# A mixture-of-experts kernel: three copies of each branch instead of five, and five branches an expert instead of eight

## The chip, the cores and the metric

The kernel runs on one core of a Trainium2 chip. TensorE (PE) multiplies matrices, VectorE (DVE), ScalarE (ACT) and GpSimd (POOL) work element by element, SyncE (SP) issues most transfers. The metric is the time of one execution on the device in microseconds, the median of several runs.

## The reference, cut to what matters

Attention with a decay writes one row of 512 values for each of 4608 tokens; each token then goes to one of eight experts, and the expert's two matrix products are done for its tokens alone:

```python
logits = x @ w_gate
expert_idx = np.argmax(logits, axis=1)
...
for e in range(E):
    mask = expert_idx == e
    xe = x[mask]
    h = np.maximum(xe @ w1[e], 0.0)      # 512 -> 1024
    ye = h @ w2[e]                       # 1024 -> 512
    out[mask] = gate_w[mask, None] * ye
```

How many tokens an expert gets is known only on the chip, since the routing depends on the data.

## The kernel before, in words

The first part of the program is the attention; the rest is the experts, one after the other. Each expert has room for CAP = 640 tokens. Expert 0 is done in a simpler way, partly beside the attention's end; experts 1 to 7 all run the same code, and the change touches these seven.

An expert from 1 to 7 has two stages. In the **up stage** (line 1421) the first product, xe @ w1, is done by a seven-product scheme for 2 x 2 blocks (Strassen's): the tokens are split in even and odd ones, 320 columns each, and the sums of blocks that the scheme needs are made beforehand (names T1 to T4, B11, B21, B22). The hidden width of 1024 is cut into four **groups** i = 0..3, and each group needs seven products s = 0..6, so an expert has 28 products, numbered 0 to 27 here (product 7i+s). A product is six matmuls of 128 x 128 weights against n columns (the values are held as a high and a low part, hence three matmuls for each of two halves of the inner dimension), so the up stage has 168 matmuls. In the **down stage** (line 1229) the second product follows in five tiles of 128 tokens with 24 matmuls of 512 columns each; the tiles of the next expert's tokens are turned between them (line 1390).

The number of columns n depends on the expert's token count. `arms` turns the count into a number from 0 to ARMS-1, TensorE loads it into a register at the start of the expert (`begin_up`), and `by_count` writes a tree of branches whose ends hold one whole copy of the same matmuls for each n:

```python
def pick(lo, hi):
    if lo == hi:
        f(HN - ARM * lo)          # one copy, with HN - ARM * lo columns
        return
    mid = (lo + hi + 1) // 2
    with self.tc.If(self.arm < mid) as branch:
        pick(lo, mid - 1)
    with branch.Else():
        pick(mid, hi)
```

Only the copy that is taken runs; the code of the others is jumped over. The first matmul that opens a bank has 320 columns in every copy (16 of the 168). With this data the experts 1 to 7 run with 320, 320, 288, 304, 256, 304 and 288 columns.

A branch comes with the products 0 to 3 of each group, and another with the products 4 to 6, so TensorE goes through eight trees an expert, with borders at the products 0, 4, 7, 11, 14, 18, 21 and 25.

The other engines turn a group's banks into the hidden layer (`after`, `end`, `last`): ACT copies bank a to p1 (line 1475) and bank g to p5 (line 1481); DVE adds u2 = b + p1 (line 1478), then u3 (1486), d (1487), g (1494); POOL adds p5 (1488); ACT takes relu of each (`relu`, line 1466, into hhw) and DVE the low part (`rest`, line 1469, into hl). They work at the full 320 columns whatever n is. Between these stand the tasks for the same engines: rounding and splitting the weights of this expert and the next (lines 1333, 1339, 1348, 1349), sums of weight blocks on POOL (1318 to 1321), loads and gathers. Every engine has its own queue, and the instructions keep the order in which the program lists them; semaphores tie the engines together. A group's last sums and relus (`ends`) are listed after the next group's first products, those of the last group at the start of the down stage.

Of the kernel before, what the change touches and what calls it, by code (L numbers as in the profile page):

```python
# [9 lines left out]
F32 = mybir.dt.float32  # L10
# [5 lines left out]
ALU = mybir.AluOpType  # L16
# [4 lines left out]
P = 128  # L21
# [3 lines left out]
D = H * HD  # L25
# [12 lines left out]
FT = FF // P  # L38
# [2 lines left out]
CA, CB = NA * P, NB * P  # L41

HN = CAP // 2
ARM, ARMS = 16, 5
XM = 2 * (KT // 2) * HN
XN = ("T2", "T1", "T4", "T3", "B22")

# [126 lines left out]
def psum(pool):  # L174
    return pool.tile([P, 512], F32, name="ps", tag="ps")
# [13 lines left out]
def attention_all(c, tc, qkT, va, vb, f, wgd, x_dram, batch_done, more_consts, extra):  # L189
# [659 lines left out]
    def run(f):  # L849
        step(f)  # L850
        order.pin()

    return run, todo


# [213 lines left out]
class Moe:  # L1069
# [69 lines left out]
    def fetch(self, e, m):  # L1139

        c, nc = self.c, self.nc
        early = e == 0 and m < NA
        gi, s = (self.idx["early"], m) if early else self.index(e, m)[::3]
        rows = self.x_dram
        if early:
            rows = rows[0 : rows.shape[0] - LATE * S]

        xg = c.rows.tile([P, D], F32R, name="xg", tag="row")
        nc.gpsimd.indirect_dma_start(
            out=xg.bitcast(F32), out_offset=None, in_=rows,  # L1150
            in_offset=bass.IndirectOffsetOnAxis(ap=gi[:, s : s + 1], axis=0),
        )
        self.xg[e, m] = xg
# [289 lines left out]
            max_val=ARMS - 1,  # L1443
        )

    def seven(self, e, i, run, tasks):

        c, nc = self.c, self.nc
        V, A, G = nc.vector, nc.scalar, nc.gpsimd
        pools = (c.ps_t, c.ps_t, c.ps_m, c.ps_v) if i % 2 == 0 else (c.ps_s,) * 3  # L1450
        a, b, g, d = [psum(p) for p in pools] + [c.ps_r] * (i % 2)
        a, b, g, d = (t[:, 0:HN] for t in (a, b, g, d))

        late = (e, i) == (1, 0)
        p1, p5, u2, u3 = (
            c.yp.tile([P, D], F32, name="y")[:, 0:HN] if late and k == 1
            else c.values["u", k] if k < 2 else self.up_.tile([P, HN], F32, name=f"u{k}")
            for k in range(4)
        )
        hh, hl = self.h[e]  # L1460

        def place(h, f, n):
            return h[:, f * (FT // 2) + i].rearrange("p (s j) -> p j s", j=2)[:, n]

        def relu(src, *at):
            A.activation(place(hh, *at), src, AF.Relu)  # L1466

        def rest(src, *at):
            V.scalar_tensor_tensor(place(hl, *at), src, 0.0, place(hh, *at).bitcast(F32),  # L1469
                                   ALU.max, ALU.subtract)  # L1470

        def after(s):
            if s == 0:
                self.ends.pop(0)()
                A.copy(p1, a)
                self.ends.pop(0)()
            elif s == 1:
                V.tensor_tensor(u2, b, p1, ALU.add)
                self.ends.pop(0)()
            elif s == 2:  # L1480
                A.copy(p5, g)  # L1481
            elif s == 4:
                relu(a, 0, 0)
                rest(a, 0, 0)
            elif s == 5:
                V.tensor_tensor(u3, b, p1, ALU.add)  # L1486
                V.tensor_tensor(d, u3, d, ALU.subtract)
                G.tensor_tensor(p5, u3, p5, ALU.add)  # L1488

        def end():  # L1490
            relu(d, 1, 0)
            if not late:
                relu(p5, 1, 1)
            V.tensor_tensor(g, g, u2, ALU.add)
            rest(d, 1, 0)

        steps = ((a, 0, 0, "B11", True), (b, 0, 1, "T2", True), (g, 0, 2, "T1", True),
                 (d, 0, 3, "T4", True), (a, 1, 0, "B21", False), (b, 1, 1, "T3", False),
                 (g, 1, 2, "B22", False))
        for some in ((0, 1, 2, 3), (4, 5, 6)):  # L1500
            run(lambda: self.by_count(
                e, lambda n: [self.product(e, i, n, *steps[s]) for s in some]))
            for s in some:
                run(lambda: after(s))
                for f in tasks.get(7 * i + s, []):
                    run(f)
        def last():
            if late:
                relu(p5, 1, 1)
            rest(p5, 1, 1)  # L1510
            rest(g, 0, 1)

        self.ends = [end, lambda: relu(g, 0, 1), last]

    def run(self, run, tasks):
        c, tc = self.c, self.tc
# [4 lines left out]
        def downs(e, ms, tasks):  # L1521
            k = 0
            for m in ms:
                for q in range(4):
                    run(lambda: self.down(e, m, (2 * q, 2 * q + 2)))
                    for f in tasks.get(k, []):
                        run(f)
                    k += 1
# [27 lines left out]
        with tc.tile_pool(name="moe_h", bufs=1) as hp, tc.tile_pool(name="moe_u", bufs=1) as up_, \  # L1556
                tc.tile_pool(name="moe_r", bufs=2) as self.wr:
            self.up_ = up_
            hl = hp.tile([P, FT * CAP], F32R, name="hl")
            h = [t.rearrange("p (f s) -> p f s", s=CAP) for t in (c.words["hh"], hl)]  # L1560
            G = self.nc.gpsimd
            for e in range(1, E):
                self.h[e] = h
                run(lambda: self.begin_up(e))
                S = lambda f, *args: T(f, e, *args)
                N = lambda f, *args: T(f, e + 1, *args)
                ups, dns = {}, {}

                def at(d, *items):
                    for k, f in items:  # L1570
                        d.setdefault(k, []).append(f)

                late = 9 if e == 1 else 1
                at(ups, (0, S(self.load_v, 0)), (0, S(self.load_v, 1)),
                   (4, S(self.round_s, 2, 1)), (6, S(self.rest_s, 2, 1, G)),
                   (late, S(self.load_v, 2)), (late, S(self.load_v, 3)),
                   (8, S(self.split_s, 3, 0)), (11, S(self.round_s, 3, 1)),
                   (13, S(self.rest_s, 3, 1, G)))
                for i, k in enumerate((15, 22, 16, 23) if e == 1 else (9, 15, 16, 22)):
                    at(ups, (k, S(self.split_v, i)))  # L1580
                if e == 1:
                    at(ups, (0, S(self.sums_s, 3)), (2, S(self.split_s, 2, 0)))
                if e + 1 < E:
                    at(ups, (9, N(self.load_s, 0)), (16, N(self.load_s, 1)),
                       (6, fetch(e + 1, 3)), (6, fetch(e + 1, 4)), (13, fetch(e + 1, 2)),
                       (20, N(self.sums_s, 0)), (20, fetch(e + 1, 0)),
                       (27, N(self.sums_s, 1)))
                    at(dns, (0, N(self.begin_t)), (0, N(self.turn_t, 3)), (0, fetch(e + 1, 1)),
                       (0, N(self.split_s, 0, 0)), (1, N(self.split_s, 0, 1)),
                       (2, N(self.load_s, 2)), (2, N(self.turn_t, 4)),  # L1590
                       (3, N(self.split_s, 1, 0)), (4, N(self.turn_t, 2)),
                       (5, N(self.split_s, 1, 1)), (6, N(self.load_s, 3)),
                       (6, N(self.turn_t, 0)), (7, N(self.sums_s, 2)),
                       (8, N(self.turn_t, 1)), (9, N(self.split_s, 2, 0)),
                       (10, N(self.split_t, "T2")), (11, N(self.split_t, "T1")),
                       (12, N(self.split_t, "T4")), (13, N(self.split_t, "T3")),
                       (14, N(self.sums_s, 3)))
                else:
                    at(ups, (27, lambda: tc.keep_in_program_order(G.drain())))
                self.ends = [lambda: None] * 3  # L1600
                for i in range(FT // 2):
                    self.seven(e, i, run, ups)
                dns.setdefault(0, [])[:0] = self.ends
                downs(e, range(NST), dns)

# [222 lines left out]
```

## Time and profile before

| | |
|---|---|
| time, median of 3 runs | 767.41 us (767.35 to 769.39) |
| the profiled execution | 766.13 us, of it a span of 764.4 us |
| PE busy | 741.7 us, 97% of the span |
| DVE, POOL, ACT busy | 541.7, 513.3 and 499.3 us |
| up stages of experts 1 to 7, together | 181.49 us |
| down stages of the same | 217.10 us |

The span is the time from the first to the last instruction that the profiler recorded; 1.7 us of the time lie outside it. "Busy" adds up the time in which an engine has an instruction in work; matmuls overlap each other in the records, so two that follow without a pause start closer together than one of them lasts.

### The profile page before, as it was taken

The page shows a single profiled execution, that of the slowest core. Times are in us where ns is not written, and L with a number is a line of the kernel's source. Part 1 is how long each engine was busy: PE and PEld are TensorE (multiplying, and loading weights), DVE is VectorE, ACT ScalarE, POOL GpSimd, SP SyncE. Part 2 cuts the span into 40 slices and gives each one's busy share as a digit, 9 for nine tenths or more (in the row PEclk, how much of TensorE's full clock was granted, in tenths as well). Part 3 has the DMA queues.
Part 4 walks back from the last instruction along what each step waited for, and adds up shares of the span by engine and source line. Part 5 has one row for each costly group of instructions (what it writes and reads, how often), then busy time and mean ns, then how long its engine had stood idle before and what let it go on. Part 6 is the DMA issues. An engine that isn't in the chain of part 4 may idle for free.

```text
span 764.4 us, 18736 instructions
## 1 busy us (share of the span) xinstructions
PE 741.7 (97%) x6464; PEld 633.3 (83%) x6464; DVE 541.7 (71%) x1596; ACT 499.3 (65%) x1319; POOL 513.3 (67%) x681
## 2 busy tenths in 40 slices
PE   9999999999999999999989999999999889999996
PEld 5888888888888887989978888988988878978985
DVE  6668898988888887627777387486585585685720
ACT  6999998999899996525555465464554554653621
POOL 6999998989898989544864475465565465565311
PEclk8999999999999999999999999999999999999998
DMA  6957787777766674333533613622632532623200
GB/s 187 222 151 211 197 215 189 204 198 212 202 197 213 200 217 139 111 117 110 182 95 111 199 53 111 206 67 90 204 96 93 170 93 83 193 83 108 77 29 34
DMA packets 78583, 112.17 MB, mean 147 GB/s; under 512 B 9327, under 2 KB 40047, under 8 KB 78448
## 3 DMA queue, kind: packets, MB, share of 16 engines
q1 hardware_dynamic: 71408, 90.38, 41.6%
q0 software_dynamic: 6400, 19.93, 8.0%
q8 instruction: 91, 1.49, 0.8%
q14 instruction: 44, 0.36, 0.2%
q10 hardware_dynamic: 640, 0.01, 0.0%
HBM read 91.26 MB, written 20.07 MB: 146 GB/s over the span
## 4 chain that ended last, share of the span: by engine, by line
PE 85%; DVE 6%; POOL 4%; issue 2%; ACT 1%; DMA 1%; SPq 0%; POOLq 0%; DVEq 0%; ACTq 0%
PE ps L1229 29%; PE ps L1421 13%; PE ps L525 11%; PE ps L402 9%; PE ps L454 8%; PE ps L436 4%; PE ps L1195 3%; PE ps L449 3%; DVE w_1w L1349 2%; DVE hl L1469 2%; PE ps L1390 1%; PE ps L616 1%; POOL u L1488 1%; POOL w L1086 1%; ACT hhw L1466 1%
## 5 line engine op out<-in xcount | busy, mean ns | idle before, releaser
L421 ACT ACTIVATE sc<-sc,nmx 128x512 f32<-128x512 f32 (+3 forms) x256 | 142.4, 559 | 5.6 <-DVE nmx L378 4.6
L1238 POOL DMA_INDIRECT out<-y,si_fast x40 | 42.9, 1072 | 118.0 <-ACT y L1237 75.0
L1229 PE MATMUL ps<-w_0w,hhw 128*128 128x512 f32 x280 | 113.4, 405 | 2.6 <-ACT hhw L1466 2.6
L1229 PE MATMUL ps<-w_0w,hl 128*128 128x512 f32 x280 | 110.7, 395 | 0.0
L1229 PE MATMUL ps<-w_1w,hhw 128*128 128x512 f32 x280 | 110.3, 394 | 0.0
L1421 PE MATMUL ps<-X_0w,w1s 128*128 128x320 f32 (+3 forms) x504 | 107.3, 304 | 0.2 <-ACT u L1481 0.2
L466 ACT COPY aT<-ps 128x512 f32<-128x512 f32 (+1 forms) x224 | 93.3, 506 | 1.9 <-PE ps L454 1.1
L329 POOL TENSOR_TENSOR hl<-raw,hl 128x640 fp32r<-128x640 f32 (+1 forms) x60 | 89.7, 1494 | 5.0
L525 PE MATMUL ps<-aT,va_t 128*64 128x256 f32 (+3 forms) x896 | 90.3, 353 | 0.0
L1421 PEld LDWEIGHTS ps<-X_0w,w1s 128*128 128x128 f32 x504 | 83.2, 191 | 0.5 <-ACT u L1481 0.4
L1237 ACT ACTIVATE y<-ps,g_fast 128x512 f32<-128x512 f32 x40 | 27.6, 689 | 81.2 <-PE ps L1229 81.2
L402 PE MATMUL ps<-hl 64*128 64x512 f32 (+1 forms) x720 | 79.8, 339 | 0.0
L525 PEld LDWEIGHTS ps<-aT,va_t 128*64 128x64 f32 x896 | 56.1, 137 | 28.5 <-issue 5.0
L1421 PE MATMUL ps<-X_1w,w1s 128*128 128x320 f32 (+3 forms) x252 | 76.0, 301 | 0.3 <-issue 0.3
L1488 POOL TENSOR_TENSOR u<-u,u 128x320 f32<-128x320 f32 x27 | 23.8, 881 | 68.3 <-DVE u L1486 60.3
L1421 PE MATMUL ps<-xa,w1s 128*128 128x320 f32 (+3 forms) x336 | 58.4, 310 | 11.0 <-issue 3.5
L378 DVE CUSTOM_DVE_ANT_0 sc<-ps,bias 128x128 f32<-128x128 f32 (+1 forms) x128 | 59.8, 486 | 10.3 <-PE ps L402 3.7
L1229 PEld LDWEIGHTS ps<-w_0w,hhw 128*128 128x128 f32 x280 | 52.5, 187 | 14.8 <-ACT hhw L1466 4.5
L1229 PEld LDWEIGHTS ps<-w_0w,hl 128*128 128x128 f32 x280 | 52.6, 188 | 14.1 <-DVE hl L1469 1.7
L1421 PEld LDWEIGHTS ps<-xa,w1s 128*128 128x128 f32 x336 | 50.2, 193 | 15.6 <-issue 4.8
L1229 PEld LDWEIGHTS ps<-w_1w,hhw 128*128 128x128 f32 x280 | 52.7, 188 | 10.1
L378 DVE CUSTOM_DVE_ANT_1 sc<-ps,bias 128x256 f32<-128x256 f32 (+1 forms) x128 | 57.7, 487 | 3.4 <-PE ps L402 3.3
(247 smaller groups left out, 1886.7 us busy)
## 6 DMA issues: line engine op xcount, KB each, us to landing
bias<-ud SPq DMA_DIRECT2D x30, 576.0 KB, 5.9
w1r<-in_w SPq DMA_DIRECT2D x112, 128.0 KB, 2.6
w<-in_w SPq DMA_DIRECT2D x28, 512.0 KB, 5.1
raw<-in_qkT SPq DMA_DIRECT2D x64, 160.0 KB, 3.6
raw<-in_qkT SPq DMA_DIRECT2D x64, 144.0 KB, 3.6
va_t<-in_va SPq DMA_DIRECT2D x32, 256.0 KB, 5.7
x_dram<-row SPq DMA_DIRECT2D x32, 256.0 KB, 2.7
wraw<-in_w SPq DMA_DIRECT2D x7, 512.0 KB, 3.9
```

The lines of the kernel that those rows point to most:

```text
L329: return eng.tensor_tensor(hl[:, 1], raws[n][:, r : r + w], hl[:, 0].bitcast(F32), ALU.subtract)
L378: red_last[:] = [V.tensor_tensor_reduce(dst, src, in1, -0.125, init, ALU.add, ALU.min, nms[n][:, col : col + 1]).ins]
L402: note(nc.tensor.matmul(pb[j][:, o : o + w], q[js], k[js], start=(i == 0), stop=(i == len(terms) - 1),))
L421: A.activation(x, x, AF.Exp, bias=nms[n][:, 5 * j + t : 5 * j + t + 1], scale=-1.0, accum_out=ssums[b][:, t, 2 * p + j : 2 * p + j + 1])
L436: note(nc.tensor.matmul(pb[half][:, 0:JW], q, k, start=(i == 0), stop=(i == len(terms) - 1),))
L454: note(nc.tensor.transpose(out.bitcast(F32R), words, c.identr[rows, rows]))
L466: copy_on = {"a": lambda o, i: A.copy(o, i), "v": lambda o, i: V.tensor_copy(o, i)}
L525: note(nc.tensor.matmul(pv[j * HD : (j + 1) * HD, q0 - qa : qb - qa], l, r, start=(blk == 0), stop=(blk == nb - 1),))
L1229: c.note(nc.tensor.matmul(py, rows(hi_, ft), w[wi], start=(ft + k == 0), stop=(ft == FT - 1 and k == 2),))
L1238: nc.gpsimd.indirect_dma_start(out=self.out, out_offset=bass.IndirectOffsetOnAxis(ap=si[:, s : s + 1], axis=0), in_=y, in_offset=None, bou ...
L1421: self.nc.tensor.matmul(bank[:, 0:cols], w[:, wi, mat, kt], x[xi][:, kt, 0:cols], start=start and k == 0, stop=k == 5, skip_group_check=True,)
L1488: G.tensor_tensor(p5, u3, p5, ALU.add)
```

## The change

The steps between the copies become 32 columns, and there are three of them: 320, 288 and 256. A count that took 304 columns takes 320 now, one that took 272 takes 288. The products 4 to 6 of a group and the products 0 to 3 of the next are put under one branch, so that an expert has five trees, with borders at 0, 4, 11, 18 and 25. The function for a group (`seven`, now `group`) only makes the steps, and a new function `sevens` runs all 28 products of an expert. What runs on the other engines after each product is as before.

```diff
@@ -41,7 +41,7 @@
 CA, CB = NA * P, NB * P
 
 HN = CAP // 2
-ARM, ARMS = 16, 5
+ARM, ARMS = 32, 3
 XM = 2 * (KT // 2) * HN
 XN = ("T2", "T1", "T4", "T3", "B22")
 
@@ -1443,7 +1443,7 @@
             max_val=ARMS - 1,
         )
 
-    def seven(self, e, i, run, tasks):
+    def group(self, e, i):
 
         c, nc = self.c, self.nc
         V, A, G = nc.vector, nc.scalar, nc.gpsimd
@@ -1452,11 +1452,11 @@
         a, b, g, d = (t[:, 0:HN] for t in (a, b, g, d))
 
         late = (e, i) == (1, 0)
-        p1, p5, u2, u3 = (
-            c.yp.tile([P, D], F32, name="y")[:, 0:HN] if late and k == 1
-            else c.values["u", k] if k < 2 else self.up_.tile([P, HN], F32, name=f"u{k}")
-            for k in range(4)
+        p1, p5 = (
+            c.yp.tile([P, D], F32, name="y")[:, 0:HN] if late and k == 1 else c.values["u", k]
+            for k in range(2)
         )
+        us = {}
         hh, hl = self.h[e]
 
         def place(h, f, n):
@@ -1475,7 +1475,8 @@
                 A.copy(p1, a)
                 self.ends.pop(0)()
             elif s == 1:
-                V.tensor_tensor(u2, b, p1, ALU.add)
+                us[2] = self.up_.tile([P, HN], F32, name="u2")
+                V.tensor_tensor(us[2], b, p1, ALU.add)
                 self.ends.pop(0)()
             elif s == 2:
                 A.copy(p5, g)
@@ -1483,34 +1484,50 @@
                 relu(a, 0, 0)
                 rest(a, 0, 0)
             elif s == 5:
+                u3 = self.up_.tile([P, HN], F32, name="u3")
                 V.tensor_tensor(u3, b, p1, ALU.add)
                 V.tensor_tensor(d, u3, d, ALU.subtract)
                 G.tensor_tensor(p5, u3, p5, ALU.add)
+            elif s == 6:
+                self.ends = [end, lambda: relu(g, 0, 1), last]
 
         def end():
             relu(d, 1, 0)
             if not late:
                 relu(p5, 1, 1)
-            V.tensor_tensor(g, g, u2, ALU.add)
+            V.tensor_tensor(g, g, us[2], ALU.add)
             rest(d, 1, 0)
 
-        steps = ((a, 0, 0, "B11", True), (b, 0, 1, "T2", True), (g, 0, 2, "T1", True),
-                 (d, 0, 3, "T4", True), (a, 1, 0, "B21", False), (b, 1, 1, "T3", False),
-                 (g, 1, 2, "B22", False))
-        for some in ((0, 1, 2, 3), (4, 5, 6)):
-            run(lambda: self.by_count(
-                e, lambda n: [self.product(e, i, n, *steps[s]) for s in some]))
-            for s in some:
-                run(lambda: after(s))
-                for f in tasks.get(7 * i + s, []):
-                    run(f)
         def last():
             if late:
                 relu(p5, 1, 1)
             rest(p5, 1, 1)
             rest(g, 0, 1)
 
-        self.ends = [end, lambda: relu(g, 0, 1), last]
+        steps = ((a, 0, 0, "B11", True), (b, 0, 1, "T2", True), (g, 0, 2, "T1", True),
+                 (d, 0, 3, "T4", True), (a, 1, 0, "B21", False), (b, 1, 1, "T3", False),
+                 (g, 1, 2, "B22", False))
+        return steps, after
+
+    def sevens(self, e, run, tasks):
+
+        groups, n = {}, 7 * (FT // 2)
+        bounds = [0] + [7 * i + 4 for i in range(FT // 2)] + [n]
+
+        def products(cols, some):
+            for k in some:
+                self.product(e, k // 7, cols, *groups[k // 7][0][k % 7])
+
+        for k0, k1 in zip(bounds, bounds[1:]):
+            some = range(k0, k1)
+            for k in some:
+                if k % 7 == 0:
+                    groups[k // 7] = self.group(e, k // 7)
+            run(lambda: self.by_count(e, lambda cols: products(cols, some)))
+            for k in some:
+                run(lambda: groups[k // 7][1](k % 7))
+                for f in tasks.get(k, []):
+                    run(f)
 
     def run(self, run, tasks):
         c, tc = self.c, self.tc
@@ -1598,8 +1615,7 @@
                 else:
                     at(ups, (27, lambda: tc.keep_in_program_order(G.drain())))
                 self.ends = [lambda: None] * 3
-                for i in range(FT // 2):
-                    self.seven(e, i, run, ups)
+                self.sevens(e, run, ups)
                 dns.setdefault(0, [])[:0] = self.ends
                 downs(e, range(NST), dns)
 
```

On TensorE, at the border between product 6 and product 7 of expert 2 before (the last rows of the copy with 256 columns, then the next tree and its copy with 320; X_0w, X_1w and xa are the tokens' blocks, w1s the weights):

```order
L1421 MATMUL ps<-X_1w,w1s 128x256
L1421 MATMUL ps<-X_0w,w1s 128x256 x2
L1421 MATMUL ps<-X_1w,w1s 128x256
L1433 UNCONDITIONAL_BRANCH
L1433 COMPARE_AND_BRANCH x2
L1421 MATMUL ps<-xa,w1s 128x320 x6
L1421 MATMUL ps<-X_0w,w1s 128x320 x2
L1421 MATMUL ps<-X_1w,w1s 128x320
L1421 MATMUL ps<-X_0w,w1s 128x320 x2
L1421 MATMUL ps<-X_1w,w1s 128x320
```

The same border in the changed kernel, inside the copy with 320 columns:

```order
L1421 MATMUL ps<-X_1w,w1s 128x320
L1421 MATMUL ps<-X_0w,w1s 128x320 x2
L1421 MATMUL ps<-X_1w,w1s 128x320
L1421 MATMUL ps<-X_0w,w1s 128x320 x2
L1421 MATMUL ps<-X_1w,w1s 128x320
L1421 MATMUL ps<-xa,w1s 128x320 x6
L1421 MATMUL ps<-X_0w,w1s 128x320 x2
L1421 MATMUL ps<-X_1w,w1s 128x320
L1421 MATMUL ps<-X_0w,w1s 128x320 x2
L1421 MATMUL ps<-X_1w,w1s 128x320
```

The jump, the compares and the copies that lay between the two products are gone; one product follows the other in the same copy.

On DVE, the first two groups of expert 2 before (u_8757 is u2 of group 0, hl the low part; each branch row is the end of a tree that holds nothing for this engine):

```order
L1478 TENSOR_TENSOR u_8757<-ps,u_96 128x320
L1433 UNCONDITIONAL_BRANCH x2
L1469 SCALAR_TENSOR_TENSOR hl<-ps,hhw 128x320
L1486 TENSOR_TENSOR u_8758<-ps,u_96 128x320
L1487 TENSOR_TENSOR ps<-u_8758,ps 128x320
L1494 TENSOR_TENSOR ps<-ps,u_8757 128x320
L1469 SCALAR_TENSOR_TENSOR hl<-ps,hhw 128x320
L1478 TENSOR_TENSOR u_8999<-ps,u_96 128x320
```

and after:

```order
L1479 TENSOR_TENSOR u_8476<-ps,u_96 128x320
L1433 UNCONDITIONAL_BRANCH
L1469 SCALAR_TENSOR_TENSOR hl<-ps,hhw 128x320
L1488 TENSOR_TENSOR u_8616<-ps,u_96 128x320
L1489 TENSOR_TENSOR ps<-u_8616,ps 128x320
L1498 TENSOR_TENSOR ps<-ps,u_8476 128x320
L1469 SCALAR_TENSOR_TENSOR hl<-ps,hhw 128x320
L1479 TENSOR_TENSOR u_8631<-ps,u_96 128x320
```

One of the two adjacent branch rows is gone, and nothing else moved; the lines have new numbers. The queues of ACT, POOL and SP differ in the same way, by the branch rows alone.

In the whole program TensorE's queue shrinks from 10,648 matmuls in all copies to 8,296, and from some 22,200 instructions to some 17,100 where a matmul's weight load is counted with it.

## Rows read from the trace of the kernel before

**Rows 1.** Part 1 of the page: busy time, share, instructions.

```profile
PE 741.7 (97%) x6464; PEld 633.3 (83%) x6464; DVE 541.7 (71%) x1596; ACT 499.3 (65%) x1319; POOL 513.3 (67%) x681
```

**Rows 2.** Who PE waited for, whole program: us in total, times, longest.

```profile
PE ps L1421 <- issue: 3.9, 3, 2.3
PE ps L1229 <- ACT hhw L1466: 2.6, 4, 0.9
```

**Rows 3.** Windows, up stages of experts 1 to 7: us; PE, PEld, DVE, ACT, POOL busy; clock.

```profile
365.81:395.18 29.37, 26.66 (x170) 26.15 (x168) 22.13 (x33) 16.33 (x30) 21.46 (x21) 0.94 0.51 162
425.54:452.75 27.21, 25.12 (x169) 24.61 (x168) 18.12 (x33) 15.78 (x29) 14.85 (x14) 1.00 0.46 147
482.56:508.10 25.54, 23.50 (x170) 22.68 (x168) 18.75 (x32) 15.64 (x29) 15.41 (x14) 1.00 0.50 151
537.59:562.04 24.45, 24.10 (x169) 23.59 (x168) 18.30 (x32) 15.30 (x29) 14.58 (x13) 1.00 0.49 154
592.52:618.97 26.45, 22.87 (x170) 22.02 (x169) 17.48 (x31) 15.33 (x29) 13.59 (x13) 0.94 0.47 142
650.06:674.27 24.21, 24.15 (x170) 23.66 (x168) 17.74 (x31) 15.18 (x29) 14.03 (x13) 1.00 0.49 152
705.05:729.31 24.26, 23.60 (x170) 22.68 (x168) 18.42 (x32) 15.40 (x29) 7.23 (x6) 1.00 0.26 85
```

**Rows 4.** Timeline of PE, experts 2 and 4: start and length, us.

```profile
425.54 1.04 PE L1421 MATMUL ps<-xa,w1s 128*128 128x320 f32 x6
...
429.05 1.04 PE L1421 MATMUL ps<-xa,w1s 128*128 128x320 f32 x6
...
540.98 0.99 PE L1421 MATMUL ps<-xa,w1s 128*128 128x304 f32 x6
...
543.49 1.00 PE L1421 MATMUL ps<-xa,w1s 128*128 128x320 f32 x6
```

**Rows 5.** Line 1433, the branches: whole program, then three single ones (min/median/max ns).

```profile
L1433 PEldq COMPARE_BRANCH  x168: 65/187/4747, 362.5 to 727.7; - x168
...
L1433 PEldq COMPARE_BRANCH  x1: 4747/4747/4747, 379.7 to 379.7; - x1
...
L1433 PEldq COMPARE_BRANCH  x1: 3669/3669/3669, 429.1 to 429.1; - x1
...
L1433 PEldq COMPARE_BRANCH  x1: 187/187/187, 444.0 to 444.0; - x1
```

**Rows 6.** Part 3 of the page: packets, MB, share of 16 engines.

```profile
q8 instruction: 91, 1.49, 0.8%
```

**Rows 7.** Timeline of PE, where it sat idle (idle and what ended it).

```profile
384.75 1.69 PE L1421 MATMUL ps<-xa,w1s 128*128 128x320 f32 x5 [2.28 <-ACT w_0w L1348]
...
398.04 0.50 PE L1229 MATMUL ps<-w_0w,hhw 128*128 128x512 f32 x1 [0.26 <-ACT hhw L1466]
...
433.05 1.14 PE L1421 MATMUL ps<-xa,w1s 128*128 128x320 f32 x6 [1.20 <-issue]
...
622.53 0.50 PE L1229 MATMUL ps<-w_0w,hhw 128*128 128x512 f32 x1 [0.95 <-ACT hhw L1466]
...
677.82 0.50 PE L1229 MATMUL ps<-w_0w,hhw 128*128 128x512 f32 x1 [0.94 <-ACT hhw L1466]
```

**Rows 8.** Timeline of DVE, then of ACT and PE, expert 4.

```profile
545.43 0.49 DVE L1478 TENSOR_TENSOR u<-ps,u 128x320 f32<-128x320 f32 x1 [0.49 <-PE ps L1421]
...
552.06 0.49 DVE L1478 TENSOR_TENSOR u<-ps,u 128x320 f32<-128x320 f32 x1 [0.39 <-ACT u L1475]
...
558.83 0.49 DVE L1478 TENSOR_TENSOR u<-ps,u 128x320 f32<-128x320 f32 x1 [0.37 <-ACT u L1475]
...
564.55 0.43 ACT L1466 ACTIVATE hhw<-ps 128x320 fp32r<-128x320 f32 x1
...
565.04 0.50 PE L1229 MATMUL ps<-w_0w,hhw 128*128 128x512 f32 x1 [0.40 <-ACT hhw L1466]
```

**Rows 9.** Timeline of DVE, expert 1, group 2.

```profile
381.46 0.49 DVE L1478 TENSOR_TENSOR u<-ps,u 128x320 f32<-128x320 f32 x1 [0.34 <-ACT u L1475]
```

## The prediction

> **What bounds the kernel now.** I read the page first: TensorE is busy for 97% of the span, DVE for 71% [rows 1]. So the time is TensorE's, and the question is where it works below its own pace. Next, its waits: in the up stage (line 1421) the largest is put down to "issue", that is to nothing the profile shows, and 2.6 us in the down stage to ACT's relu [rows 2]. Then the pace. Twenty-four matmuls of 320 columns take 429.05 - 425.54 = 3.51 us, 146.3 ns each; eighteen of 304 take 543.49 - 540.98 = 2.51 us, 139.4 ns [rows 4]. So 16 columns are worth 6.9 ns, and I extend this to 132.5 ns at 288 and 118.7 at 256. An up stage of 168 matmuls (16 always at 320) should then take 24.6 us at 320 columns, 23.5 at 304, 22.5 at 288 and 20.4 at 256. The windows show 29.4, 27.2, 25.5, 24.5, 26.5, 24.2 and 24.3 us, 181.5 in all [rows 3], against 2 x 24.6 + 2 x 23.5 + 2 x 22.5 + 20.4 = 161.6. Some **20 us are lost** in seven up stages, most of it in experts 1, 2, 3 and 5, and the two stages with the largest losses have a mean granted clock of 0.94.
>
> The loss sits at the branches. A branch takes 0.19 us in the median, but 3.67 us at 429.07 and 4.75 at 379.70 [rows 5]. The first was met when 18 matmuls were still queued, since product 4 started at 429.05 [rows 4]; 18 x 0.146 = 2.6 us of cover, and TensorE sat idle for 1.20 us before product 7 at 433.05, released by "issue" [rows 7]. At 384.75 the profile names ACT, but the branch of 4.75 us ended 0.3 us before, so I read this gap as the same thing. [...] What the branch waits for must be its code: the instruction queue q8 fetched 1.49 MB in 91 packets [rows 6], 16.4 KB each. The program has some 22,200 TensorE instructions, so a packet holds about 244, and an expert of 2,060 needs 8.4 of them, more than one for each of its eight trees.
>
> **The change, part by part.**
>
> *Fewer branches and less code.* An expert's code falls by (22,200 - 17,100)/7 = 730 instructions to 1,330, 5.5 packets. Between two borders inside the up stage lie 42 matmuls now, not 18 and 24 by turns: 6.1 us at 320 columns, 5.0 at 256. A packet must be there within this time and the cover of 18 matmuls, 8.7 us down to 7.1; today within 2.6 + 2.6 us at the short trees. The worst branch took 4.75 us. So I take the code losses to zero. The bound from the other side is that only the stalls at the three borders that go (7, 14, 21) vanish.
>
> *More columns.* Experts 4 and 6 go from 304 to 320 columns in 152 matmuls each: 2 x 152 x 6.9 ns = 2.1 us of TensorE's time.
>
> *The other engines.* Their queues lose 21 branch rows each and keep everything else; each wait, theirs and TensorE's, is for the same instruction as before. Nothing is queued differently, so these rows cost and give nothing that I count.
>
> *What is late next.* If TensorE alone counted, 20 - 2.1 = 18 us would come back. But the hidden layer must come off the banks, and this work is 320 columns wide whatever n is. Expert 4, which lost least but one, shows its pace: DVE's u2 starts at 545.43, 552.06 and 558.83 for groups 1, 2 and 3, the last relu starts at 564.55, and TensorE, which had been idle for 0.40 us in the down stage, goes on at 565.04 [rows 8]. The steps are 6.63, 6.77 and 6.21 us, 19.6 from group 1 to that matmul, and a group's seven products at 320 columns take 42 x 0.146 = 6.1. So **DVE and ACT are slower than an unhindered TensorE**; group 1's u2 still waits for product 8, and from there the chain runs at its own pace. It is now hidden by the lost time in experts 2, 3 and 5.
>
> The point to compare is that matmul of the down stage. Group 1's u2 came 7.84 us after the start in expert 4 [rows 3, 8]; 54 matmuls lie before it, hence 8.2 at 320 columns, 7.5 at 288, 6.8 at 256. Adding 19.6:
>
> - 320 columns (experts 2, 4, 6): 27.8 us after the expert's start. Expert 4 is there at 565.04 - 537.59 = 27.45 now, expert 6 at 677.82 - 650.06 = 27.76 [rows 3, 7, 8]. Expert 2 has no wait there; its stage of 27.2 plus the 2.6 us which expert 4's matmul came after its stage's end without the 0.40 idle gives 29.8. So +0.4, 0 and -2.0.
> - 288 (expert 3): 27.1 against 25.5 + 2.6 = 28.1, -1.0. Expert 7 has no next expert's work on DVE's tail and little to give: 24.3 + 2.6 = 26.9 now, -0.4 by TensorE's wait for group 3.
> - 256 (expert 5): 26.4 against 622.53 - 592.52 = 30.0 [rows 3, 7], -3.6.
> - Expert 1 is special: DVE has 22.1 us of work there, others 18 [rows 3]. Its u2 of group 2 starts at 381.46 and waits for ACT, not for TensorE [rows 9], 15.65 us after the start, and nothing before it hangs on the stall. With expert 4's last two steps it would be at 15.65 + 6.77 + 6.21 = 28.6; half of the 3.8 us of extra work may still lie behind, 30.5 at worst. I take 29.4, nearer the first since most of the extra stands early. Now it is 398.04 - 365.81 = 32.2 [rows 7], so -2.8 (-1.7 to -3.6).
>
> Sum: -2.8 - 2.0 - 1.0 + 0.4 - 3.6 + 0 - 0.4 = **-9.4 us**. The added columns thus cost 0.4 and not 2.1, because TensorE waits there anyway. The other end of this term is 0 waiting, -18 us. I shave 0.4 for waits that TensorE will meet on the way, in the fourth group of expert 5 above all. The profiled execution has 766.13 us; minus 9.0 gives 757.1. It lies 1.3 below the median of the runs, so I forecast **758.4 us**.
>
> [...]
>
> **The rivals.**
>
> 1. *TensorE runs through.* The chain of DVE and ACT gives way, because its steps are partly waits for a late TensorE. Against: in expert 4, with an almost unhindered TensorE, ACT ended DVE's waits for groups 2 and 3, and they are 0.4 us of each 6.7 [rows 8]. 767.4 - 18 = 749.4, with half of it 754.
> 2. *Kept borders keep their stalls* (18 in experts 1 and 3, 25 in expert 5). Expert 1 then keeps the 2.28 us at its border 18 [rows 7]; if experts 3 and 5 keep some 0.8 each, the sum is -9.0 + 3.9 = -5.1, 762.3. For it: late packets may come from the loads that fill the queues then. Against: a packet has twice the time.
> 3. *Slower.* A tree of seven products is some 258 instructions, more than one packet of 244, so the jump from the first copy's end lands a whole packet further on. If the code is asked for only when the jump is met, each of the 28 inner jumps loses what the one at 429.07 lost, 433.05 - 431.69 = 1.36 us (18 matmuls after 429.05 end at 431.69): 38 us instead of 20, plus 2.1, 787. It decides from 0.64 us a jump on. Against: today's trees of four products in five copies are about a packet long too, and the median branch takes 0.19 us [rows 5].
> 4. *No gain that shows*: stalls vanish and the same time is waited for in the down stage, or 1 and 2 us are lost elsewhere: 765 to 769.
>
> [...]
>
> **How the numbers follow.** The forecast's case, 756.5 to 761, has 0.62; rival 2 (761 to 764.5) 0.17; rival 1 (749 to 756.5) 0.10; rival 4 0.07; rival 3 or another new wait 0.04. A change of 0.3%, 2.3 us, is about what a measurement of this kernel tells from none. Faster takes the first three, 0.89; same 0.07; slower 0.04. The range from 753.5 to 764.5 takes in the half of rival 1 and all of rival 2.
>
> **What would show it.** Right: no branch above some 2.6 us with an idle TensorE behind it, the up stages at 24.6 to 25.5 us for 320 columns and near 23 for the others, no clock below 1 in them; q8 near 70 packets; TensorE's waits for the relu in the down stage grow from 2.6 to 5 us or more; DVE's u2 6.6 to 6.8 us apart in all experts. Wrong: long branches at the borders 11, 18 and 25 (rival 2 or 3), or u2 closer together than 6.5 us at 320 columns (rival 1).

## The result and the profile after

The changed kernel takes **759.63 us** (median of 4 runs, 758.27 to 761.37); the kernel before took 768.04 us beside it (767.35 to 769.39). The ratio is 0.989, 95% interval 0.9863 to 0.9917: 8.4 us faster, against a forecast of 758.4. The profiled execution of after has 760.25 us, a span of 758.5; that of before had 766.13, so these two differ by 5.9 us only. Line numbers are now 1475 (p1), 1479 (u2), 1482 (p5 copy), 1488, 1489, 1490 (u3, d and POOL's p5).

The page of the changed kernel, parts 1 and 3, against [rows 1, 6]:

```profile
PE 739.9 (98%) x6464; PEld 632.8 (83%) x6464; DVE 542.4 (72%) x1596; ACT 499.2 (66%) x1319; POOL 514.8 (68%) x681
...
q8 instruction: 71, 1.16, 0.7%
```

Its waits of PE (us, times, longest), against [rows 2]:

```profile
PE ps L1229 <- ACT hhw L1466: 5.9, 7, 1.7
PE ps L1421 <- ACT u L1475: 3.0, 5, 1.0
```

Its branches, whole program (min/median/max ns), against [rows 5]:

```profile
L1433 PEldq COMPARE_BRANCH  x80: 65/177/617, 363.1 to 721.9; - x80
```

"Issue" is gone from the waits of these two lines, and no branch takes longer than 0.62 us, where one took 4.75. In its place stand waits for ACT: 5.9 us for the relu, 3.0 for p1. The windows of the up stages after (us; PE, PEld, DVE, ACT, POOL busy; clock), against [rows 3]:

```profile
366.40:391.50 25.10, 24.86 (x169) 24.60 (x168) 20.59 (x33) 16.04 (x30) 20.63 (x20) 1.00 0.57 188
424.52:449.12 24.60, 24.60 (x169) 24.60 (x168) 18.13 (x32) 15.43 (x29) 14.55 (x13) 1.00 0.48 154
479.63:503.22 23.59, 23.00 (x170) 22.62 (x168) 17.79 (x30) 15.26 (x29) 13.90 (x13) 1.00 0.51 161
534.15:558.75 24.60, 24.60 (x169) 24.59 (x168) 18.14 (x32) 15.43 (x29) 14.53 (x13) 1.00 0.48 152
589.29:612.40 23.11, 21.34 (x169) 20.59 (x168) 17.69 (x30) 15.20 (x29) 13.79 (x13) 1.00 0.52 162
643.71:668.31 24.60, 24.60 (x170) 24.60 (x168) 17.84 (x31) 15.35 (x29) 14.25 (x13) 1.00 0.45 146
699.17:722.75 23.58, 22.98 (x170) 22.62 (x168) 17.77 (x31) 15.22 (x29) 7.26 (x6) 1.00 0.25 82
```

They add up to 169.2 us instead of 181.5, every one at a clock of 1.00. The four with 320 columns stand at 24.6, TensorE's own pace, but for 0.5 us in expert 1. Expert 5, whose 256 columns would allow 20.4, stays at 23.1. Timeline of PE after, where each down stage waits for the relu (idle in brackets), against [rows 7]:

```profile
395.83 0.64 PE L1229 MATMUL ps<-w_0w,hhw 128*128 128x512 f32 x1 [1.72 <-ACT hhw L1466]
...
452.16 0.50 PE L1229 MATMUL ps<-w_0w,hhw 128*128 128x512 f32 x1 [0.42 <-ACT hhw L1466]
...
506.88 0.50 PE L1229 MATMUL ps<-w_0w,hhw 128*128 128x512 f32 x1 [1.03 <-ACT hhw L1466]
...
561.79 0.50 PE L1229 MATMUL ps<-w_0w,hhw 128*128 128x512 f32 x1 [0.42 <-ACT hhw L1466]
...
616.16 0.50 PE L1229 MATMUL ps<-w_0w,hhw 128*128 128x512 f32 x1 [1.14 <-ACT hhw L1466]
...
671.63 0.50 PE L1229 MATMUL ps<-w_0w,hhw 128*128 128x512 f32 x1 [0.70 <-ACT hhw L1466]
...
725.49 0.50 PE L1229 MATMUL ps<-w_0w,hhw 128*128 128x512 f32 x1 [0.47 <-ACT hhw L1466]
```

All seven experts wait at this matmul now. Timeline of DVE, then ACT, in expert 4 after, against [rows 8]:

```profile
542.33 0.49 DVE L1479 TENSOR_TENSOR u<-ps,u 128x320 f32<-128x320 f32 x1 [0.64 <-PE ps L1421]
...
548.80 0.49 DVE L1479 TENSOR_TENSOR u<-ps,u 128x320 f32<-128x320 f32 x1 [0.38 <-ACT u L1475]
...
555.56 0.49 DVE L1479 TENSOR_TENSOR u<-ps,u 128x320 f32<-128x320 f32 x1 [0.36 <-ACT u L1475]
...
560.92 0.49 ACT L1466 ACTIVATE hhw<-u 128x320 fp32r<-128x320 f32 x1 [0.83 <-POOL u L1490]
561.31 0.44 ACT L1466 ACTIVATE hhw<-ps 128x320 fp32r<-128x320 f32 x1
```

From group 1's u2 to the matmul at 561.79 it is 6.47 + 6.76 + 6.23 = 19.5 us; the forecast took 19.6.

### The profile page after: what moved, and what is told of

It is laid out like the page before. It is cut to its first block, busy times and chain, and to the rows that moved or that the text cites. A ratio compares the mean times of both kernels' runs of the same rounds, so it can differ in the third digit from the quotient of the medians.

```text
span 758.5 us, 18648 instructions
## 1 busy us (share of the span) xinstructions
PE 739.9 (98%) x6464; PEld 632.8 (83%) x6464; DVE 542.4 (72%) x1596; ACT 499.2 (66%) x1319; POOL 514.8 (68%) x681
## 4 chain that ended last, share of the span: by engine, by line
PE 72%; DVE 15%; POOL 6%; ACT 3%; issue 2%; DMA 0%; POOLq 0%; DVEq 0%; ACTq 0%
PE ps L1229 27%; PE ps L525 11%; PE ps L402 9%; PE ps L454 7%; PE ps L1421 5%; DVE w_1w L1349 5%; PE ps L436 4%; DVE hl L1469 4%; POOL u L1490 3%; PE ps L449 2%; PE ps L1195 2%; ACT hhw L1466 2%; DVE w1s L1339 2%; POOL w L1086 1%; DVE u L1488 1%
## 5 line engine op out<-in xcount | busy, mean ns | idle before, releaser
L1421 PE MATMUL ps<-X_0w,w1s 128*128 128x320 f32 (+2 forms) x504 | 107.4, 303 | 0.2 <-ACT u L1482 0.2
L1237 ACT ACTIVATE y<-ps,g_fast 128x512 f32<-128x512 f32 x40 | 27.6, 691 | 81.8 <-PE ps L1229 76.2
L1421 PE MATMUL ps<-X_1w,w1s 128*128 128x320 f32 (+2 forms) x252 | 75.8, 301 | 0.0
L1421 PE MATMUL ps<-xa,w1s 128*128 128x320 f32 (+2 forms) x336 | 56.2, 302 | 3.0 <-ACT u L1475 3.0
L1339 DVE TENSOR_TENSOR w1s<-w1r,w1s 128x1024 fp32r<-128x1024 f32 (+1 forms) x42 | 49.1, 1183 | 11.9 <-ACT w1s L1333 10.2
```

The lines of the kernel that those rows point to most:

```text
L1339: (eng or self.nc.vector).tensor_tensor(lo, raw, hi.bitcast(F32), ALU.subtract)
L1421: self.nc.tensor.matmul(bank[:, 0:cols], w[:, wi, mat, kt], x[xi][:, kt, 0:cols], start=start and k == 0, stop=k == 5, skip_group_check=True,)
```

## The experiments

Theory: the copies that are jumped over cost time through the instruction code that must be fetched; once that is gone, the chain on DVE, ACT and POOL sets the end of the up stage. Rivals: the number of trees is what cost, or TensorE itself is the limit. Medians in us, ratios to the kernel before beside each (768 to 770). "Long branches" are the single records of line 1433 over 0.7 us, added up; packets an expert are worked out as in the prediction. Packets, branches and up stages are those of the one profiled execution of each run, the times are medians.

| run | copies x trees | packets an expert | q8 packets | long branches | up stages | time | ratio, interval |
|---|---|---|---|---|---|---|---|
| before | 5 x 8 | 8.4 | 91 | 26, 58.7 | 181.5 | 768.0 | 1 |
| after | 3 x 5 | 5.5 | 71 | none | 169.2 | 759.6 | 0.989 (0.986 to 0.992) |
| copies3 | 3 x 8 | 5.7 | 72 | none | 169.1 | 759.5 | 0.987 (0.983 to 0.992) |
| four8 | 4 x 8 | 7.1 | 81 | 11, 22.1 | 171.3 | 762.1 | 0.989 (0.984 to 0.994) |
| four5 | 4 x 5 | 7.1 | 81 | 9, 23.2 | 179.2 | 764.2 | 0.993 (0.990 to 0.996) |
| fuse5 | 5 x 5 | 8.4 | 91 | 17, 49.2 | 196.4 | 778.4 | 1.010 (1.006 to 1.015) |
| dead5 | 5 x 5 | 8.4 | 91 | 18, 50.0 | 194.4 | 780.4 | 1.014 (1.010 to 1.019) |
| one | 1 x 0 | | 52 | none | 172.7 | 761.1 | 0.989 (0.985 to 0.993) |

**Each half alone.** The kernel before with three copies:

```diff
-ARM, ARMS = 16, 5
+ARM, ARMS = 32, 3
```

> The kernel before with three copies 32 columns apart, its eight trees an expert kept. Theory (the code that is fetched is what cost): an expert's code falls to about 1,390 instructions, 5.7 packets, nearly as in the changed kernel, and the stalls go: 758 to 761 us, some 70 to 75 packets in q8, no branch above 1.5 us. Rival (the number of trees is what cost): 56 trees lost some 20 us, 0.36 us each, all 56 are still there, and two experts have 16 columns more: 767 to 769 us. In between, 762 to 765 us: both count.

759.52 us. Its branches, whole program:

```profile
L1433 PEldq COMPARE_BRANCH  x128: 65/176/421, 361.3 to 718.5; - x128
```

It records 48 branches more than the changed kernel, and none takes longer than 0.42 us. The whole gain comes with the three copies; fewer trees give nothing that these runs can tell. The other half alone, the changed kernel with five copies:

```diff
-ARM, ARMS = 32, 3
+ARM, ARMS = 16, 5
```

> The changed kernel with the five copies 16 columns apart of before, in five trees an expert. Theory (code that is fetched): as much code an expert as before, about 2,050 instructions, 8.4 packets; the longer tree gives more cover between borders, but the jump from the first copy's end passes over some 340 instructions, more than one packet of 244: stalls stay, 764 to 775 us, some 90 packets in q8, branches above 3 us. Rival (the number of trees): 35 trees instead of 56 give back three eighths of 20 us, 7.5 us, 760 us or less since experts 4 and 6 keep 304 columns.

778.4 us: it is slower than the kernel before, by more than was expected. Timeline of PE in expert 2 of this run, behind the border at product 11:

```profile
440.27 1.14 PE L1421 MATMUL ps<-xa,w1s 128*128 128x320 f32 x6 [1.19 <-ACT w_0w L1348]
```

and the branch ahead of it:

```profile
L1433 PEldq COMPARE_BRANCH  x1: 3653/3653/3653, 436.3 to 436.3; - x1
```

The profile names ACT for the idle time, but the branch ran from 436.3 until 439.95, and the next tree's compares, then product 11, followed at once. ACT's rounding ended only shortly before, at 439.88, but it isn't what product 11 needs: in the changed kernel product 11 of expert 2 starts at 434.20, while ACT works at the same rounding until 435.18. Such stalls stand at the borders 11 and 18 in most experts.

**Only dead code.** Five copies again, but with the changed kernel's widths, so that TensorE executes the same matmuls as in after:

```diff
-ARM, ARMS = 32, 3
+ARM, ARMS = 16, 5
...
-                f(HN - ARM * lo)
+                f(HN - 2 * ARM * (lo // 2))
```

> The changed kernel with five copies of which two pairs are alike (320, 320, 288, 288, 256 columns): TensorE executes the same matmuls as in the changed kernel, and only the code that is jumped over grows. Theory (code that is fetched): as in the run with five trees of five copies, 764 to 775 us, 5 us or more above the changed kernel. Rival (number of trees, or columns): as the changed kernel, 759 to 761 us.

780.4 us, above the 764 to 775 that were expected. Instructions that never run cost some 20 us. Its branches, with the longest of 6.1 us:

```profile
L1433 PEldq COMPARE_BRANCH  x105: 65/219/6102, 363.6 to 737.2; - x105
```

**Amount of code, or length of a jump?** The kernel before with `ARM, ARMS = 16, 4`:

> The kernel before with four copies 16 columns apart (320 to 272), eight trees an expert. About 1,730 instructions an expert, 7.1 packets, half way between the kernels without stalls (5.5 and 5.7) and those with (8.4); the longest jump passes over 144 instructions, 0.6 of a packet, less than the 168 of the changed kernel. If the amount of code decides: about half of the 59 us that branches of more than 0.7 us took before, 20 to 35 us, and 762 to 765 us. If the length of the jump decides: no long branch, 758 to 760 us.

The changed kernel with `ARM, ARMS = 16, 4`:

> The changed kernel with four copies 16 columns apart, five trees an expert: the same 7.1 packets an expert, but the longest jump passes over 252 instructions, just over one packet. If the amount of code decides: stalls about half of those with five copies, 765 to 771 us. If the length of the jump decides: as with five copies, 772 to 780 us.

762.1 us, as expected if the amount of code decides, and 764.2, 0.8 below what was expected then. With the same code an expert both have the same sum of long branches, 22 and 23 us, somewhat less than half of the 49 to 59 at 8.4 packets, though their longest jumps pass over 144 and 252 instructions. The run with jumps of 144 has long branches, the changed kernel with jumps of 168 has none: the length of the jump does not decide, the code an expert does. (At 5.5 packets the waiting is not wholly nothing: a single branch of 0.7 to 1.0 us stands in expert 3 of three of the later runs with the changed kernel's copies.) What the same waiting costs does depend on the trees. In few, long waits (mostly 3 to 5 us, at two borders an expert, in fuse5) more lies beyond the cover than in many short ones: 49 us of branches cost fuse5 more than 59 cost the kernel before (up stages of 196.4 and 181.5 us).

**The packets themselves.** So far they were counted in total only; the traces have each with its time. Packets of the instruction queue in the up stage of expert 2, before (425.54 to 452.75) and after (424.52 to 449.12), then in the branch of fuse5 from 436.30 to 439.95:

```profile
q8 instruction: 7, 0.11, 1.5%
...
q8 instruction: 3, 0.05, 0.9%
...
q8 instruction: 1, 0.02, 2.2%
```

In the five kernels of the table that have long branches, every one of the 81 ends 1.2 to 1.5 us after a packet of q8 has ended (the 26 of the kernel before 1.20 to 1.51). That ties the wait to the code more directly than the totals do. No two of these packets begin less than 2.96 us apart (3.05 in the kernel before).

**No columns saved.** One copy at 320 columns, no branch:

```diff
-ARM, ARMS = 32, 3
+ARM, ARMS = 32, 1
```

> The changed kernel with one copy at 320 columns and no branch in the up stage. TensorE has more work: 152 matmuls of 32 columns more (2.1 us) in experts 3 and 7 each, of 64 more (4.2 us) in expert 5, 8.4 us in all. Theory (the chain on DVE and ACT sets the end of the up stage): only the 54 matmuls ahead of group 1's u2 count, 0.7 us in experts 3 and 7, 1.4 in expert 5, 2.8 at most: 760 to 763 us, with u2 still 6.5 to 6.8 us apart and less waiting for the relu. Rival (TensorE sets it): 767 to 769 us.

761.1 us. Windows of experts 3 and 5 in this run:

```profile
480.97:505.57 24.60, 24.60 (x169) 24.60 (x168) 18.15 (x32) 15.40 (x29) 14.53 (x13) 1.00 0.49 159
591.24:615.84 24.60, 24.60 (x169) 24.60 (x168) 18.14 (x32) 15.41 (x29) 14.53 (x13) 1.00 0.49 152
```

8.4 us more of TensorE's work by the pace at 320, 288 and 256 columns make 1.5 us by the medians, and nothing by the ratios to the kernel before beside each (0.989 both): two copies of three save almost nothing, because expert 5 spends with waiting most of what it saves in columns. In after it reaches the matmul of the down stage 26.9 us after its start, with one copy 27.6.

**The tail of the chain.** One gather moved:

```diff
-                       (20, N(self.sums_s, 0)), (20, fetch(e + 1, 0)),
+                       (20, N(self.sums_s, 0)), (27, fetch(e + 1, 0)),
```

> The changed kernel with one gather of the next expert's tokens moved from behind product 20 to behind product 27 on POOL's queue, behind the last p5. Theory (the end of the up stage is the chain of DVE, ACT and POOL; in experts 2 to 6 its last link is the p5 that waits on POOL's queue, since ACT's relu waits 0.83 us for POOL there): that relu comes up to 0.83 us earlier, and TensorE's waits of 0.42, 1.03, 0.42, 1.14 and 0.70 us in the down stages of experts 2 to 6 shrink by as much: 3.2 us, 756 to 757 us. Rival (DVE alone is the last link): no change, 759 to 760 us. Second rival (the tokens now come late for their turn in the down stage): slower than 760 us.

758.1 us (755.3 to 760.4; ratio 0.987, 0.984 to 0.990): between theory and no change. Its waits of PE:

```profile
PE ps L1421 <- ACT u L1475: 3.0, 5, 1.0
PE ps L1229 <- ACT hhw L1466: 2.9, 4, 1.7
PE ps L1229 <- DVE hl L1469: 2.0, 6, 0.4
```

The wait for the relu halves as expected, but 2.0 us of it come back as waits for DVE's low part, the next link. Then the split of w2:

```diff
-                for i, k in enumerate((15, 22, 16, 23) if e == 1 else (9, 15, 16, 22)):
+                for i, k in enumerate((15, 22, 16) if e == 1 else (9, 15, 16)):
                     at(ups, (k, S(self.split_v, i)))
+                at(dns, (0, S(self.split_v, 3)))
```

> The changed kernel with the last of an expert's four splits of w2 (1.05 us on ACT, 1.2 to 1.4 us on DVE) moved from the fourth group to the start of the down stage. Theory as before: in experts 2 to 6 the last p5 is held by POOL's queue, so nothing is won there; in expert 1, where DVE does two splits in a row (3.05 us) and POOL is not the last, the wait of 1.72 us falls by 1.2 or more and the slow matmuls behind it go (1.6 us); in expert 7 0.47 us: 756 to 757 us. Rival (DVE alone is the last link): 5.9 us of waiting and the 1.6 behind it go, 752 to 753 us. Second rival (the split is now late for the fourth pair of matmul rows in the down stage or pushes the turns): 760 us or more.

755.8 us (ratio 0.985, 0.983 to 0.988), a little more than the theory gave. Timeline of POOL in expert 4, the changed kernel:

```profile
557.14 1.72 POOL L1321 TENSOR_TENSOR w1r<-w1r 128x256 f32<-128x256 f32 x1
```

and this run:

```profile
553.80 0.73 POOL L1321 TENSOR_TENSOR w1r<-w1r 128x256 f32<-128x256 f32 x1
```

POOL's sum ahead of p5 took 1.72 us beside DVE's split (556.90 to 558.26), and 0.73 without it, 0.99 us less. The two links are not independent, which the theory had overlooked: p5 comes an us earlier in experts 2 to 6 too (in expert 5 counted from its last u2). In expert 1 the wait is 0.84 us and the clock behind it stays at 1.00. Both moves together:

> The changed kernel with both moves, the split of w2 and the gather. Theory: both last links are loosened, p5 can start 1.05 us earlier in experts 2 to 6, and nearly all of TensorE's 5.9 us of waiting for the relu goes, with the 1.6 us behind the wait of expert 1: 752 to 754 us, and below it TensorE's own pace. Rival (the two moves push other work into the down stage, whose turns then make TensorE wait): 756 us or more.

**752.8 us** (752.1 to 755.2; ratio 0.982, 0.979 to 0.984), 6.8 below the changed kernel. Its waits of PE for results in the up and down stages:

```profile
PE ps L1421 <- ACT u L1475: 3.3, 5, 1.0
PE ps L1229 <- DVE hl L1469: 1.1, 3, 0.4
PE ps L1421 <- ACT u L1482: 0.3, 2, 0.2
```

The relu is gone from them; 1.1 us are left for DVE's low part. The same two moves in the kernel before:

> The kernel before with the same two moves. Theory (before, the chain is covered by the waits for code in most experts): TensorE waits 2.6 us for the relu here, so 1 to 2.5 us are won, less than half of what the two moves win in the changed kernel: 765 to 767 us if the kernel before has 768. Rival (the chain limits both kernels alike): 6 to 7 us are won here too, 761 to 762 us.

764.6 us (ratio 0.996, 0.993 to 0.998): 3.3 us, a little above the expectation, half of what they win after. The chain hid behind the code there in part.

**What limits then.** One copy and both moves:

> One copy at 320 columns together with both moves (the split of w2 and the gather). Theory (in the changed kernel the chain of DVE, ACT and POOL hid TensorE's extra columns; the two moves loosen it): now the columns count, 2.1 us in experts 3 and 7 each and 4.2 less the 2.3 us of waits in expert 5, some 5 to 6 us above the kernel with both moves, 757 to 760 us, against 1.5 us without the moves. Rival (the columns cost little whatever the chain does): 753 to 755 us.

754.2 us (ratio 0.981, 0.976 to 0.986): the expectation of 5 to 6 us more was wrong: it is 1.4 by the medians, and nothing by the ratios. The moves loosen the chain's end, not its pace; expert 5 of the run with both moves shows it in PE's timeline:

```profile
597.58 0.98 PE L1421 MATMUL ps<-xa,w1s 128*128 128x256 f32 x6 [0.97 <-ACT u L1475]
...
604.31 0.98 PE L1421 MATMUL ps<-xa,w1s 128*128 128x256 f32 x6 [0.96 <-ACT u L1475]
```

These two are 6.73 us apart, the step of u2; with 256 columns TensorE still waits for p1 at each group, and its stage takes 24.3 us against 24.6 with 320 columns. Not all of that is the pace: in after the stage took 23.1. With the moves POOL's first p5 of this expert stands behind a store of the expert before it that starts 5.6 us into the stage (1.2 in after), and group 1's u2 comes 8.4 us after the start, not 7.2. The last run tried to shorten that step:

```diff
-                   (8, S(self.split_s, 3, 0)), (11, S(self.round_s, 3, 1)),
+                   (8, S(self.round_s, 3, 0)), (11, S(self.round_s, 3, 1)),
+                   (13, S(self.rest_s, 3, 0, G)),
...
-                for i, k in enumerate((15, 22, 16) if e == 1 else (9, 15, 16)):
+                for i, k in enumerate((15, 22, 16) if e == 1 else (9, 10, 16)):
```

> Both moves, and DVE relieved further: the low part of the last w1 block (1.2 us) goes to POOL behind product 13, and the second split of w2 from product 15 to 10, so that DVE has one split between the u2 of groups 2 and 3 instead of two. Theory: what is left of TensorE's waits for p1, about 1 us at each of two groups of expert 5 and less in experts 1, 3 and 7, 3.3 us in all, goes: 750 to 752 us. Rival (POOL, now with 2.5 us more ahead of its p5, becomes the last): 754 us or more.

771.7 us (ratio 1.005, 1.002 to 1.007), 19 more than the run with both moves; the rival's direction was right, but neither expectation named what the rows show. Timeline of ACT, then DVE, expert 4 of this run:

```profile
547.43 1.05 ACT L1348 CAST w_0w<-w 128x1024 fp32r<-128x1024 f32 x1 [1.29 <-DVE w_1w L1349]
...
546.17 1.23 DVE L1349 TENSOR_TENSOR w_1w<-w,w_0w 128x1024 fp32r<-128x1024 f32 x1 [1.11 <-ACT w_0w L1348]
548.51 1.23 DVE L1349 TENSOR_TENSOR w_1w<-w,w_0w 128x1024 fp32r<-128x1024 f32 x1 [1.12 <-ACT w_0w L1348]
```

The first two splits share a tile (`w2_part` takes it by i // 2), so ACT rounds the second only when DVE is done with the first, and DVE waits for each rounding, which the w1 part used to cover. The u2 of groups 1 and 2 come 8.8 us apart instead of 6.5. This is read from the rows and the kernel; no run tests the two moves of this last edit apart, and POOL's low part, the other one, may have a share.

## Why the prediction was right, step by step

- **Code losses to zero**: right, as the branches and the clock show. That a jump waits for its code is now shown: the run with dead code changes only what is jumped over (and the depth of the trees with it, 105 branches for 80), and every long branch ends 1.2 to 1.5 us after a packet has.
- **Why they vanish**: half wrong. The forecast gave weight to the 42 matmuls between borders and the longer time for a packet. Fewer trees did not help, and with five copies they harm. The fall from 8.4 to 5.5 packets did all that these runs can tell. That the number came out right in spite of this is luck: the change holds both halves, and the one that the forecast also leaned on gives nothing.
- **More columns cost 0.4, not 2.1**: experts 4 and 6 resume 0.2 us later each than before, and one copy for all costs 1.5 us at most instead of 8.4.
- **The chain comes next**: the points of the forecast, from an expert's start to the matmul above:

| expert | 1 | 2 | 3 | 4 | 5 | 6 | 7 |
|---|---|---|---|---|---|---|---|
| before, as the forecast took it | 32.2 | 29.8 | 28.1 | 27.45 | 30.0 | 27.76 | 26.9 |
| before, in the trace | 32.2 | 29.7 | 28.0 | 27.45 | 30.0 | 27.8 | 26.4 |
| forecast | 29.4 | 27.8 | 27.1 | 27.8 | 26.4 | 27.8 | 26.5 |
| after | 29.4 | 27.6 | 27.2 | 27.6 | 26.9 | 27.9 | 26.3 |

 To the first row the differences add up to -9.2 us, the forecast's to -9.4. But the forecast had read experts 2, 3 and 7 from expert 4's distance, 0.1 to 0.5 us late; the rows of before for them are

```profile
455.20 0.39 PE L1229 MATMUL ps<-w_0w,hhw 128*128 128x512 f32 x1
...
510.56 0.39 PE L1229 MATMUL ps<-w_0w,hhw 128*128 128x512 f32 x1
...
731.40 0.47 PE L1229 MATMUL ps<-w_0w,hhw 128*128 128x512 f32 x1
```

 and to the trace the differences add up to -8.4: expert 5 gave 0.5 less than forecast, expert 7 nothing. Behind these points 1.9 us are lost again, 1.2 of them in expert 1, and expert 1 begins 0.6 us later, which leaves the 5.9 between the profiled executions, where the forecast had 9.0. The medians differ by 8.4, because before was profiled in an execution 1.9 below its median and after in one 0.6 above: that the time came out 1.2 us from the forecast is in part luck, that the chain sets the points is not.
- **Expert 1** resumes where it was forecast, but in this execution gives part of it back, which no step had: after its wait of 1.72 us TensorE ran for 3.4 us at a mean granted clock of 0.53. Windows of after, behind that wait and later:

```profile
395.83:399.25 3.42, 3.42 (x8) 2.58 (x9) 2.95 (x9) 2.31 (x5) 3.09 (x4) 0.53 0.00 0
399.88:404.00 4.12, 4.12 (x22) 3.40 (x22) 2.87 (x8) 2.87 (x7) 1.01 (x1) 1.00 0.68 187
```

 The eight matmuls from 395.83 on are 0.43 us apart instead of 0.235, 1.6 us. The low clock of 0.94 in the up stages of experts 1 and 5 [rows 3] is gone; in the kernel before it stood at 0.50 in both for a while (windows 384.85 to 388.10, behind the idle 2.28 us of [rows 7], and 599.90 to 603.10) and at 1.00 around the first of them (380.00 to 384.70, 388.30 to 392.00).
- **Rivals.** TensorE does not run through (1): from group 1 on u2 stays 6.5 us apart or more in every expert, in expert 5 with its 256 columns 6.76. (The sign was 6.6 to 6.8 in all experts; the steps are 6.47 to 7.41, and at 320 columns the first of them, 6.47 to 6.49 in experts 2, 4 and 6, lies just below the 6.5 that was to speak for this rival, the second at 6.75 to 7.05.) The kept borders keep nothing (2). The mechanism of (3), a jump that waits for code and stops TensorE, is real (in fuse5 a branch of 3.65 us, with 1.19 us of idle TensorE behind it), but the prediction had the length wrong: the jump from the first copy's end passes over two copies of 84 instructions, 0.7 of a packet and not a whole one. The waiting is what the five copies in five trees do, 19 us above the changed kernel, and three copies are below the onset of the losses, which lies between 5.7 and 7.1 packets an expert (no branch over 0.42 us in copies3, 22.1 us of long ones in four8).

The length of a jump doesn't say where the long branches come: with jumps over 168 instructions after has none (0.62 us the longest), with jumps over 144 at most four8 has 11 (22.1 us). Why the waiting starts where it does is left open: neither where a packet's border falls in a copy nor the order of fetches was varied by itself.

## What to carry over

Copies of code that are jumped over were not free here (780.4 us with the dead ones, 759.6 without): count the instruction packets in a stretch against its time, look for single long branches where the median looks harmless (0.22 us with dead code, the longest 6.1), and test with dead code alone. Before cutting columns, see whether the engines that empty the banks have the same pace at every width; here two widths more than one were worth 1.5 us at most. When a stall goes, look for the last link that it covered and move what stands ahead of it: two tasks moved in the order gave 6.8 us, nearly as much again as the change.

## What the runs showed of the hardware beyond that

- The same wait in front of expert 1's down stage, 1.72 to 1.73 us, was followed by 3.4 us at a mean clock of 0.53 in after, 0.57 in the run with the gather moved, 0.72 with one copy and 1.00 with three copies in eight trees. So the wait alone doesn't say whether the clock falls; after waits of 0.84 (the run with the split moved) and 1.14 us (expert 5 of after) it did not.
- Expert 1 began between 363.89 and 369.85 us in the profiled executions, though nothing ahead of it differs in what it does: single spans can't settle 2 us here, medians or stretches from the start of an expert can.
